# Decay factors of gated linear attention: one scan over logarithms of gates and exponentials, in place of two scans

## The chip, the cores and the metric

The kernel runs on one core of one Trainium2 chip, as one program. The metric is the device time of one execution in microseconds (us); the median over several executions is used. A core has five engines that each work through their own instructions in order: TensorE (PE in the profile, with its weight loads shown apart as PEld), VectorE (DVE), ScalarE (ACT), GpSimd (POOL) and SyncE (SP, which here only issues transfers). They wait for one another through semaphores.

## The reference

Four batches, eight heads, 768 time steps, 48 channels per head. First a gated linear attention, head by head; then, on its output with the heads laid side by side (768 x 384 per batch), a low-rank mixing over time and a two-layer network over channels.

```python
f = 1.0 / (1.0 + np.exp(-f_logit))
for t in range(S):
    state = f[:, :, t, :, None] * state + np.einsum('bhd,bhe->bhde', k[:, :, t], v[:, :, t])
    y[:, :, t] = np.einsum('bhd,bhde->bhe', q[:, :, t], state)
...
h = xt @ U @ V                      # xt: x with time and channels exchanged
u = x + h.transpose(0, 2, 1)
out = u + np.maximum(u @ w_ch1, 0.0) @ w_ch2
```

Everything is in 32-bit floats. The gates f lie between 0 and 1, one for each time step and channel.

## The kernel before

**Tiling.** A unit is a pair of heads of one batch: 16 units, numbered n = 0 to 15, four per batch. Each head takes 64 of the 128 partitions (48 channels and padding), time runs along the free dimension. The 768 steps are cut into 12 chunks of 64. Within a chunk the recurrence is written as matrix products: keys are multiplied by X, the product of the gates from the step behind theirs to the end of the chunk; queries by Y, the reciprocal of that product; scores of queries and keys, masked to the past, times values give the part from within the chunk. Between chunks a state of 48 x 48 per head is carried, scaled per chunk by the product of all its gates.

**Steps of a unit.** The function `prepare` makes X, Y, keys and queries. Units 0 to 3 (batch 0) get them from logarithms: ScalarE makes log(1 + exp(-logit)), TensorE sums it over the rest of each chunk (line 835), ScalarE takes exponentials (lines 852 to 856), and a copy (line 857) keeps the chunks' products. Units 4 to 15 (batches 1 to 3) do otherwise:

- `gates` (line 859): logits are turned so that time runs along the free dimension, by TensorE into PSUM for units 4 and 5 (line 777), by VectorE for the others (line 754, into the slice `late[6]`); ScalarE takes the sigmoid (lines 863 and 871) into a buffer `fz` whose first column of each chunk stays 0, and the sigmoid of those first columns into `f0` (lines 864 and 872). Then the load of the logits two units on is issued.
- `keep` (line 874): VectorE scans backwards over time, X[t] = f[t+1] * X[t+1] + ends[t] (line 876), then four short operations on 128 x 12 (lines 881 to 886): a copy of each chunk's product into `least`, a bound, a reciprocal into `starts`, and the chunk's whole product in `whole`.
- `keys` (line 888): the keys are turned and multiplied by X.
- `read` in `prepare`, called `read_back` where the order is written: VectorE scans forwards, Y[t] = f[t] * Y[t-1] + starts[t] (line 894).
- `queries`: the queries are turned and multiplied by Y.

The function `attend` then makes, for each unit, `kept` (keys turned back, lines 1002 to 1006, and `spread`, line 1012, which copies the chunk products to 48 columns each), `states` (line 1026, evicted by ScalarE in line 1034), `scan` (the states from chunk to chunk, on VectorE, line 1051, copied by GpSimd in line 1057 or by ScalarE in line 1055), `scores` (line 975, masked by VectorE in line 988), `read` (queries times states, line 1069, and a two-column copy `seen` on ScalarE, line 1076, which the next step waits for) and `inner` (scores times values into the same PSUM tile, line 1087, evicted by ScalarE in line 1093).

**The mixer** of a batch runs beside the attention of the next one: `ch1` (line 300) multiplies by the first weights, 12 matmuls of 256 columns into one of two PSUM banks (`ps_mm`), and ScalarE evicts with Relu (line 335); `ch2` (line 355) or a scheme with seven products (line 389) multiplies by the second weights. In the last batches a scheme with fewer products (line 495) needs many sums on VectorE (line 204, and line 929 for sums of weights).

**Weights** arrive as 64-bit words and are made into 32-bit floats while batch 0's mixer begins: two operations on ScalarE (lines 91 and 92), three on VectorE (lines 98 to 100), one addition on GpSimd (line 101) per piece.

**The order.** TensorE's instructions run in the order in which the program writes them. On VectorE and ScalarE that holds too for what is written from line 1183 to line 1306, which is batch 0, batch 1 and the first steps of unit 9's round. Instructions outside it, and all of GpSimd's, are put in order by a scheduler, which takes an instruction when, in its own model of the run, its inputs are there and its engine is free; so they may run ahead of others that stand earlier in the program. The main loop of batch 0's mixer (lines 1286 to 1292) puts behind each piece of 12 matmuls one piece of weights and then one step of the attention: gates(4), keep(4), keys(4) and so on. Later (function `steps`, line 1128), the round of unit n is: inner(n-2), scores(n-1), kept(n); from n = 7 on read_back(n) and queries(n); gates, keep and keys of n+1; then read(n-1), states(n), scan(n), with pieces of the mixer spread between by the function `Fill`.

Of the kernel before, what the change touches and what calls it, by code (L numbers as in the profile page):

```python
# [10 lines left out]
F32 = mybir.dt.float32  # L11
# [3 lines left out]
AF = mybir.ActivationFunctionType  # L15
# [549 lines left out]
def factored_path(ctx, tc, q, k, v, f_logit, moe_U, moe_V, moe_w_ch1, moe_w_ch2, out, ok):  # L565
# [135 lines left out]
    for s in range(2):  # L701
        half = causal[s * C : (s + 1) * C, :]
        nc.gpsimd.affine_select(out=half, in_=half, compare_op=ALU.is_ge, fill=0.0, base=0,
                                pattern=[[1, C]], channel_multiplier=-1)
    ends = late[:, 3, :]
    nc.vector.memset(ends, 0.0)
    nc.vector.memset(ends.rearrange("p (c t) -> p c t", t=C)[:, :, C - 1], 1.0)
    starts = other[:, 3, :]
    nc.vector.memset(starts, 0.0)
    fz = [const.tile([P, S + 1], F32, name=f"fz{i}") for i in range(2)]  # L710

    kz = [const.tile([P, C + S], F32, name=f"kz{i}") for i in range(2)]
    for i in range(2):
        nc.gpsimd.memset(kz[i][:, 0:C], 0.0)
    least = const.tile([P, NU, NCH], F32, name="least")

    wholes = [const.tile([P, NCH], F32, name=f"whole{i}") for i in range(2)]
    added = const.tile([P, D * NCH + 1], F32, name="added")
    nc.gpsimd.memset(added[:, 0:1], 0.0)
    for i in range(2):  # L720
        nc.gpsimd.memset(wholes[i][:, 0:1], 0.0)

    U = const.tile([P, NBL, R], F32, name="U")
    V = const.tile([P, (NBL * R + P - 1) // P, P], F32, name="V")
# [22 lines left out]
    def backwards(t, first, n):  # L747

        a = t[:, first : first + 1]
        return bass.AP(a.tensor, a.offset, [list(a.ap[0]), [-1, n]])  # L750

    def turned(t, src_tile):

        nc.vector.transpose(
            t.rearrange("p (c i) -> p c i", i=NB), src_tile.rearrange("p (c d) -> p c d", d=NB),
        )
# [3 lines left out]
    def prepare(n):  # L760
# [2 lines left out]
        T = units[n] = {}  # L763
        b = n // HP
        r, f = raw[n % 2], fz[n % 2]
        by_chunk = f[:, 0:S].rearrange("p (c t) -> p c t", t=C)

        def follow(nm):

            if n >= HP and n + 2 < NU:  # L770
                load(n + 2, nm)

        def on_tensor(nm):

            pt = ps_big.tile([P, 2, 512], F32, name="pt", tag="big")
            for c in range(NBL):
                nc.tensor.transpose(  # L777
                    pt[:, 2 * c // NBL, c % (NBL // 2) * P : (c % (NBL // 2) + 1) * P],
                    nat[n % 2][nm][:, c].rearrange("p h d -> p (h d)"), ident,
                )  # L780
            return pt[:, :, 0 : G * C].rearrange("p a (c t) -> p a c t", t=C)

        def halves(t):
            return t[:, 0:S].rearrange("p (a c t) -> p a c t", a=2, t=C)
# [55 lines left out]
        def keep_logs():  # L840
            def blocks_of(t):
                return t.rearrange("p (a c t) -> p a c t", a=2, t=P)

            T["X"], T["Y"] = late[:, 4 + n % 2, :], fz[n % 2][:, 0:S]
            of_least = least[:, n, :].rearrange("p (a c s) -> p a c s", a=2, s=2)
            if n == 0:
                parts = [(slice(a, a + 1), t) for a, t in enumerate(T["sums"])]
            else:
                parts = [(slice(0, 2), T["both"])]
            parts = [(a, t[:, :, 0 : NBL // 2 * (P + 2)].rearrange("p a (c t) -> p a c t", t=P + 2)) for a, t in parts]  # L850
            for a, sums in parts:
                nc.scalar.activation(blocks_of(T["X"])[:, a], sums[:, :, :, 0:P], AF.Exp, scale=-1.0)
            for a, sums in parts:
                nc.scalar.activation(blocks_of(T["Y"])[:, a], sums[:, :, :, 0:P], AF.Exp)
            for a, sums in parts:
                nc.scalar.activation(of_least[:, a], sums[:, :, :, P : P + 2], AF.Exp, scale=-1.0)
            nc.scalar.copy(wholes[n % 2][:, 1:NCH], least[:, n, 1:NCH])

        def gates():
            f0 = T["f0"] = two.tile([P, NCH], F32, name="f0")  # L860
            if n < TURNED:
                pt = on_tensor("f")
                nc.scalar.activation(halves(f)[:, :, :, 1:C], pt[:, :, :, 1:C], AF.Sigmoid)
                nc.scalar.activation(f0.rearrange("p (a c) -> p a c", a=2), pt[:, :, :, 0], AF.Sigmoid)
                follow("f")
                return
            fT = late[:, 6, :]
            turned(fT, r["f"])
            follow("f")
            fv = fT.rearrange("p (c t) -> p c t", t=C)  # L870
            nc.scalar.activation(by_chunk[:, :, 1:C], fv[:, :, 1:C], AF.Sigmoid)  # L871
            nc.scalar.activation(f0, fv[:, :, 0], AF.Sigmoid)

        def keep():
            X = T["X"] = late[:, 4, :]
            nc.vector.tensor_tensor_scan(  # L876
                backwards(X, S - 1, S), backwards(f, S, S), backwards(ends, S - 1, S), 0.0,
                ALU.mult, ALU.add,
            )
            X0 = X.rearrange("p (c t) -> p c t", t=C)[:, :, 0]  # L880
            nc.vector.tensor_copy(least[:, n, :], X0)
            X1 = two.tile([P, NCH], F32, name="X1")
            nc.vector.tensor_single_scalar(X1, X0, LEAST, ALU.max)
            nc.vector.reciprocal(starts.rearrange("p (c t) -> p c t", t=C)[:, :, 0], X1)
            whole = wholes[n % 2]
            nc.vector.tensor_tensor(whole[:, 1:NCH], T["f0"][:, 1:NCH], X0[:, 1:NCH], ALU.mult)

        def keys():
            operand("k", "X")
# [1 line left out]

        def read():
            Y = T["Y"] = late[:, 5, :]
            nc.vector.tensor_tensor_scan(Y, f[:, 0:S], starts, 0.0, ALU.mult, ALU.add)  # L894

        def queries():
            operand("q", "Y")
# [59 lines left out]
    def attend(n):  # L957
# [50 lines left out]
                spread()  # L1008

        def spread():  # L1010
            whole = T["whole"] = one.tile([P, D, NCH], F32, name="whole")
            nc.scalar.copy(whole, wholes[n % 2].unsqueeze(1).broadcast_to((P, D, NCH)))

        def halves_of(n):
            return [slice(0, D // 2), slice(D // 2, D)] if n == HP - 1 else [slice(0, D)]
# [23 lines left out]
        def scan():  # L1039

            st = T["st"] = two.tile([P, NCH, D], F32, name="st")
            by_e = "p (e c) -> p c e"
            if b == 0:
                states = st.rearrange("p c e -> p (c e)")
                T["st"] = states.rearrange(by_e, c=NCH)
            else:
                states = added[:, 0 : D * NCH]
            with tc.high_priority(offset=2 * AHEAD):
                for e in halves_of(n):
                    of = slice(e.start * NCH, e.stop * NCH)  # L1050
                    nc.vector.tensor_tensor_scan(  # L1051
                        states[:, of], added[:, of], T["whole"].rearrange("p e c -> p (e c)")[:, of], 0.0, ALU.add, ALU.mult
                    )
                if b == B - 1:
                    nc.scalar.copy(st, states.rearrange(by_e, c=NCH))
                elif b:
                    nc.gpsimd.tensor_copy(st, states.rearrange(by_e, c=NCH))  # L1057
# [125 lines left out]
    with tc.manual_schedule(engines={nc.vector.engine, nc.scalar.engine}):  # L1183
# [91 lines left out]
        m.before[4][1]()  # L1275
        ch1_of(0, 0, (0, 2), (1, 2))
        loads = loads[early + 3 :]
        for t in fz:
            nc.vector.memset(t[:, 0:S].rearrange("p (c t) -> p c t", t=C)[:, :, 0], 0.0)
            nc.vector.memset(t[:, S : S + 1], 0.0)  # L1280

        start = m.before[5:]

# [411 lines left out]
```

## Time and profile before

| | |
|---|---|
| time, median of 3 executions | 466.25 us (465.5 to 466.81) |
| span of the profiled execution, first to last instruction | 463.2 us |
| matmuls | 5639, busy 455.2 us |
| VectorE | 585 instructions, busy 351.4 us |
| ScalarE | 323 instructions, busy 170.4 us |
| GpSimd | 56 instructions, busy 48.5 us |
| granted TensorE clock, mean | 0.999 |

The profile is of one execution. A row of the timeline has start, duration (both in us), engine, line, operation, what is written and read, the number of instructions merged, and in brackets how long the engine was idle before and what released it. A row of the groups has line, engine, operation, tiles, shapes and count, then busy time in us, the mean time of one in ns, and the idle time before. A row of the windows has, for each engine, busy time and number of instructions in a stretch. Busy time of matmuls comes from modelled ends. The time of the runs lies 3.05 us above the span of the profile; that part is outside of what the profile shows.

### The profile page before, as it was taken

To read this page: it belongs to the slowest core of one execution; us is meant where nothing else is said; L and a number is where in the kernel's file an instruction comes from. 1 tells how busy PE (TensorE), PEld (TensorE's weight loads), DVE (VectorE), ACT (ScalarE), POOL (GpSimd) and SP (SyncE) were. 2 spreads that over 40 slices of the span, in tenths; PEclk is the share of its full clock that TensorE was granted. 3 is DMA by queue.
4 is the path that set the end of the run, shared out by engine and by line. 5 is a ranking of instruction groups with operands and counts; after the bars stand their busy time and mean duration, and the time that the engine had idled before them with its cause. 6 is when DMAs were issued, how large, how long until landed. Compare 5 with 4: busy or idle time off the path is not lost.

```text
span 463.2 us, 13016 instructions
## 1 busy us (share of the span) xinstructions
PE 455.2 (98%) x5639; PEld 394.5 (85%) x5639; DVE 351.4 (76%) x585; ACT 170.4 (37%) x323; POOL 48.5 (10%) x56
## 2 busy tenths in 40 slices
PE   8999999999999999999999999999999999999997
PEld 5886888875666578999898888899989999999996
DVE  6778788979999677676765559977797887858652
ACT  6785776562333143323322323451412311212200
POOL 2002445634112001010000000000000000000000
PEclk9999999999999999999999999999999999999999
DMA  9959997577777604504633030100000000000001
GB/s 194 186 139 212 227 217 180 150 119 103 124 113 118 107 18 53 78 1 89 77 52 74 14 61 4 28 3 21 18 1 1 35 1 23 13 1 35 1 36 39
DMA packets 148583, 34.35 MB, mean 74 GB/s; under 512 B 136934, under 2 KB 146982, under 8 KB 148518
## 3 DMA queue, kind: packets, MB, share of 16 engines
q1 hardware_dynamic: 147718, 33.29, 37.1%
q8 instruction: 46, 0.75, 0.7%
q10 hardware_dynamic: 800, 0.15, 0.2%
q14 instruction: 19, 0.16, 0.1%
HBM read 28.70 MB, written 4.72 MB: 72 GB/s over the span
## 4 chain that ended last, share of the span: by engine, by line
PE 80%; DVE 11%; ACT 3%; DMA 2%; issue 2%; SPq 2%; DVEq 0%; ACTq 0%
PE pw L389 27%; PE pz L300 21%; PE pp L495 12%; PE po L355 5%; PE y L1069 2%; PE sc L975 2%; PE ds L1026 2%; PE y L1087 2%; PE pt L1002 1%; SPq L661 1%; DVE late L894 1%; PE pt L777 1%; DVE late L876 1%; PE pt L835 1%; DMA other<-in_f_logit_dram 1%
## 5 line engine op out<-in xcount | busy, mean ns | idle before, releaser
L300 PE MATMUL pz<-uT,w 128*128 128x256 f32 x492 | 111.5, 382 | 0.3
L300 PEld LDWEIGHTS pz<-uT,w 128*128 128x128 f32 x492 | 91.7, 190 | 12.9 <-ACT uT L289 0.6
L389 PE MATMUL pw<-zw,w_raw 128*128 128x192 f32 x216 | 38.0, 329 | 0.0
L389 PE MATMUL pw<-w,z_all 128*128 128x192 f32 x216 | 37.3, 327 | 0.0
L335 ACT ACTIVATE z_all<-pz 128x512 f32<-128x512 f32 x33 | 19.6, 598 | 45.1 <-PE pz L300 44.7
L389 PEld LDWEIGHTS pw<-w,z_all 128*128 128x128 f32 x216 | 35.3, 190 | 0.5
L389 PEld LDWEIGHTS pw<-zw,w_raw 128*128 128x128 f32 x216 | 35.1, 190 | 0.6 <-issue 0.3
L101 POOL TENSOR_TENSOR w<-w_y,w_r 128x384 int32<-128x384 int32 x24 | 31.5, 1311 | 37.0 <-DVE w_y L100 22.5
L876 DVE TENSOR_TENSOR_SCAN late<-fz,late 128x768 f32<-128x768 f32 x12 | 21.1, 1755 | 9.4 <-ACT fz L871 9.3
L488 ACT ACTIVATE other<-other 128x512 f32<-128x512 f32 x18 | 11.3, 630 | 40.3 <-DVE other L204 40.3
L355 PE MATMUL po<-w,zw 128*128 128x384 f32 x72 | 25.2, 495 | 0.0
L355 PE MATMUL po<-w,z_all 128*128 128x384 f32 x72 | 24.7, 493 | 0.0
L1057 POOL COPY st<-added 128x576 f32<-128x576 f32 x8 | 12.4, 1556 | 113.8 <-DVE added L1051 113.8
L988 DVE TENSOR_TENSOR A<-sc,causal 128x768 f32<-128x768 f32 x16 | 15.2, 953 | 8.5 <-PE sc L975 8.5
L355 PEld LDWEIGHTS po<-w,zw 128*128 128x128 f32 x72 | 13.2, 190 | 9.6 <-issue 0.8
L894 DVE TENSOR_TENSOR_SCAN late<-fz,other 128x768 f32<-128x768 f32 x12 | 21.0, 1750 | 0.2
L355 PEld LDWEIGHTS po<-w,z_all 128*128 128x128 f32 x72 | 13.3, 190 | 8.9 <-DVE o L204 0.6
L488 ACT ACTIVATE z_all<-z_all 128x512 f32<-128x512 f32 x12 | 7.6, 631 | 34.1 <-DVE z_all L204 34.1
L1034 ACT COPY added<-ds 48x576 f32<-48x576 f32 (+2 forms) x29 | 17.8, 619 | 4.5 <-PE ds L1026 4.1
L495 PE MATMUL pp<-v_nat,late 128*128 128x128 f32 x152 | 19.1, 275 | 0.0
L1069 PEld LDWEIGHTS y<-st,qT 48*64 48x64 f32 x704 | 13.6, 137 | 6.2 <-issue 4.5
L98 DVE TENSOR_SCALAR w_y<-w_y 128x384 f32<-128x384 f32 (+3 forms) x27 | 12.1, 449 | 8.8 <-ACT w_y L91 8.8
(233 smaller groups left out, 872.1 us busy)
## 6 DMA issues: line engine op xcount, KB each, us to landing
w_raw<-in_moe_w_ch_dram SPq DMA_DIRECT2D x18, 384.0 KB, 3.6
out_dram<-o SPq DMA_DIRECT2D x17, 192.0 KB, 1.9
v_nat<-in_v_dram SPq DMA_DIRECT2D x16, 144.0 KB, 3.8
v_nat<-in_v_dram SPq DMA_DIRECT2D x32, 72.0 KB, 3.5
zw<-in_moe_w_ch_dram SPq DMA_DIRECT2D x6, 384.0 KB, 5.1
out_dram<-o SPq DMA_DIRECT2D x14, 96.0 KB, 2.2
w<-in_k_dram SPq DMA_DIRECT2D x4, 288.0 KB, 4.1
w<-in_q_dram SPq DMA_DIRECT2D x4, 288.0 KB, 4.2
```

The costliest lines, as they stand in the source:

```text
L101: nc.gpsimd.tensor_tensor(dst.bitcast(I32), shaped(y.bitcast(I32)), shaped(r), ALU.add)
L300: nc.tensor.matmul(pm[:, i * 2 * P : (i + 1) * 2 * P], lhsT=w1[:, m, o : o + P], rhs=uT[a][:, m, :], start=(m == 0), stop=(m == NDC - 1))
L335: nc.scalar.activation(z[a, c][:, k : k + 2, :].rearrange("p i t -> p (i t)"), pm, AF.Relu)
L355: nc.tensor.matmul(pm, lhsT=z[a, i // NI][:, i % NI, s * P : (s + 1) * P], rhs=w2[:, i, :], start=(i == 0), stop=(i == NFC - 1))
L389: nc.tensor.matmul(W["pm"][:, n * HM : (n + 1) * HM], lhsT=lhs[:, i, :], rhs=rhs[:, i, :], start=(i == 0), stop=(i == NI - 1))
L488: nc.scalar.activation(dst, dst, AF.Relu, scale=float(SIGNS[n]))
L495: nc.tensor.matmul(pm[:, i, r * P : (r + 1) * P], lhsT=room["w"](wn)[:, r * P : (r + 1) * P], rhs=x_node(a, xn), start=((xn, wn) == of[0]) ...
L876: nc.vector.tensor_tensor_scan(backwards(X, S - 1, S), backwards(f, S, S), backwards(ends, S - 1, S), 0.0, ALU.mult, ALU.add,)
L894: nc.vector.tensor_tensor_scan(Y, f[:, 0:S], starts, 0.0, ALU.mult, ALU.add)
L988: nc.vector.tensor_tensor(T["A"], sc[:, :, 0 : NBL * C].rearrange("p h (c i) -> p h c i", i=C), causal.unsqueeze(1).unsqueeze(1).broadcast ...
L1034: nc.scalar.copy(added[r, 1:].rearrange("p (e c s) -> p e c s", c=NBL, s=2)[:, e], ds[r, :, 0 : NBL * D].rearrange("p s (c e) -> p e c s", ...
L1069: nc.tensor.matmul(o(c % 2, par, c // 2), lhsT=T["q"][rows[par], chunk[c]], rhs=T["st"][rows[par], c, :], start=(c <= 2), stop=False, skip ...
```

## The change

For units 4 to 15 the gates stay logarithms until after the scan. GpSimd first bounds the logits from below by -40, in place. They are turned as before; ScalarE takes exp(-logit) and then log(1 + ...), in place, over all 768 columns. One backward scan on VectorE, in place, sums these over the rest of each chunk (`within` is 1, and 0 in each chunk's last column). ScalarE then takes X as the exponential of minus the sum, the chunks' products straight into `least`, and, in place of the second scan, Y as the exponential of the sum. The bound, the reciprocal and the product on 128 x 12 are gone; last columns of X and Y are set to 1 once. In batch 0 the copy of line 857 is gone, since `spread` reads `least`.

```diff
--- before.py
+++ after.py
@@ -702,23 +702,20 @@
         half = causal[s * C : (s + 1) * C, :]
         nc.gpsimd.affine_select(out=half, in_=half, compare_op=ALU.is_ge, fill=0.0, base=0,
                                 pattern=[[1, C]], channel_multiplier=-1)
-    ends = late[:, 3, :]
-    nc.vector.memset(ends, 0.0)
-    nc.vector.memset(ends.rearrange("p (c t) -> p c t", t=C)[:, :, C - 1], 1.0)
-    starts = other[:, 3, :]
-    nc.vector.memset(starts, 0.0)
-    fz = [const.tile([P, S + 1], F32, name=f"fz{i}") for i in range(2)]
+    within = late[:, 3, :]
+    nc.vector.memset(within, 1.0)
+    nc.vector.memset(within.rearrange("p (c t) -> p c t", t=C)[:, :, C - 1], 0.0)
+    fz = [const.tile([P, S], F32, name=f"fz{i}") for i in range(2)]
 
     kz = [const.tile([P, C + S], F32, name=f"kz{i}") for i in range(2)]
     for i in range(2):
         nc.gpsimd.memset(kz[i][:, 0:C], 0.0)
     least = const.tile([P, NU, NCH], F32, name="least")
 
-    wholes = [const.tile([P, NCH], F32, name=f"whole{i}") for i in range(2)]
+    whole = const.tile([P, D, NCH], F32, name="whole")
+    nc.gpsimd.memset(whole[:, :, 0], 0.0)
     added = const.tile([P, D * NCH + 1], F32, name="added")
     nc.gpsimd.memset(added[:, 0:1], 0.0)
-    for i in range(2):
-        nc.gpsimd.memset(wholes[i][:, 0:1], 0.0)
 
     U = const.tile([P, NBL, R], F32, name="U")
     V = const.tile([P, (NBL * R + P - 1) // P, P], F32, name="V")
@@ -763,7 +760,9 @@
         T = units[n] = {}
         b = n // HP
         r, f = raw[n % 2], fz[n % 2]
-        by_chunk = f[:, 0:S].rearrange("p (c t) -> p c t", t=C)
+
+        def by_chunk(t):
+            return t.rearrange("p (c t) -> p c t", t=C)
 
         def follow(nm):
 
@@ -841,7 +840,7 @@
             def blocks_of(t):
                 return t.rearrange("p (a c t) -> p a c t", a=2, t=P)
 
-            T["X"], T["Y"] = late[:, 4 + n % 2, :], fz[n % 2][:, 0:S]
+            T["X"], T["Y"] = late[:, 4 + n % 2, :], f
             of_least = least[:, n, :].rearrange("p (a c s) -> p a c s", a=2, s=2)
             if n == 0:
                 parts = [(slice(a, a + 1), t) for a, t in enumerate(T["sums"])]
@@ -854,36 +853,25 @@
                 nc.scalar.activation(blocks_of(T["Y"])[:, a], sums[:, :, :, 0:P], AF.Exp)
             for a, sums in parts:
                 nc.scalar.activation(of_least[:, a], sums[:, :, :, P : P + 2], AF.Exp, scale=-1.0)
-            nc.scalar.copy(wholes[n % 2][:, 1:NCH], least[:, n, 1:NCH])
 
         def gates():
-            f0 = T["f0"] = two.tile([P, NCH], F32, name="f0")
+            raw_f = nat[n % 2]["f"][:, :, :, 0:D] if n < TURNED else r["f"]
+            nc.gpsimd.tensor_single_scalar(raw_f, raw_f, FLOOR, ALU.max)
             if n < TURNED:
-                pt = on_tensor("f")
-                nc.scalar.activation(halves(f)[:, :, :, 1:C], pt[:, :, :, 1:C], AF.Sigmoid)
-                nc.scalar.activation(f0.rearrange("p (a c) -> p a c", a=2), pt[:, :, :, 0], AF.Sigmoid)
-                follow("f")
-                return
-            fT = late[:, 6, :]
-            turned(fT, r["f"])
+                nc.scalar.activation(halves(f), on_tensor("f"), AF.Exp, scale=-1.0)
+            else:
+                turned(f, r["f"])
+                nc.scalar.activation(f, f, AF.Exp, scale=-1.0)
             follow("f")
-            fv = fT.rearrange("p (c t) -> p c t", t=C)
-            nc.scalar.activation(by_chunk[:, :, 1:C], fv[:, :, 1:C], AF.Sigmoid)
-            nc.scalar.activation(f0, fv[:, :, 0], AF.Sigmoid)
+            nc.scalar.activation(f, f, AF.Ln, bias=1.0)
 
         def keep():
+            nc.vector.tensor_tensor_scan(
+                backwards(f, S - 1, S), backwards(within, S - 1, S), backwards(f, S - 1, S), 0.0, ALU.mult, ALU.add,
+            )
             X = T["X"] = late[:, 4, :]
-            nc.vector.tensor_tensor_scan(
-                backwards(X, S - 1, S), backwards(f, S, S), backwards(ends, S - 1, S), 0.0,
-                ALU.mult, ALU.add,
-            )
-            X0 = X.rearrange("p (c t) -> p c t", t=C)[:, :, 0]
-            nc.vector.tensor_copy(least[:, n, :], X0)
-            X1 = two.tile([P, NCH], F32, name="X1")
-            nc.vector.tensor_single_scalar(X1, X0, LEAST, ALU.max)
-            nc.vector.reciprocal(starts.rearrange("p (c t) -> p c t", t=C)[:, :, 0], X1)
-            whole = wholes[n % 2]
-            nc.vector.tensor_tensor(whole[:, 1:NCH], T["f0"][:, 1:NCH], X0[:, 1:NCH], ALU.mult)
+            nc.scalar.activation(by_chunk(X)[:, :, 0 : C - 1], by_chunk(f)[:, :, 1:C], AF.Exp, scale=-1.0)
+            nc.scalar.activation(least[:, n, :], by_chunk(f)[:, :, 0], AF.Exp, scale=-1.0)
 
         def keys():
             operand("k", "X")
@@ -891,7 +879,7 @@
 
         def read():
             Y = T["Y"] = late[:, 5, :]
-            nc.vector.tensor_tensor_scan(Y, f[:, 0:S], starts, 0.0, ALU.mult, ALU.add)
+            nc.scalar.activation(by_chunk(Y)[:, :, 0 : C - 1], by_chunk(f)[:, :, 1:C], AF.Exp)
 
         def queries():
             operand("q", "Y")
@@ -1008,8 +996,7 @@
                 spread()
 
         def spread():
-            whole = T["whole"] = one.tile([P, D, NCH], F32, name="whole")
-            nc.scalar.copy(whole, wholes[n % 2].unsqueeze(1).broadcast_to((P, D, NCH)))
+            nc.scalar.copy(whole[:, :, 1:], least[:, n, 1:].unsqueeze(1).broadcast_to((P, D, NCH - 1)))
 
         def halves_of(n):
             return [slice(0, D // 2), slice(D // 2, D)] if n == HP - 1 else [slice(0, D)]
@@ -1049,7 +1036,7 @@
                 for e in halves_of(n):
                     of = slice(e.start * NCH, e.stop * NCH)
                     nc.vector.tensor_tensor_scan(
-                        states[:, of], added[:, of], T["whole"].rearrange("p e c -> p (e c)")[:, of], 0.0, ALU.add, ALU.mult
+                        states[:, of], added[:, of], whole.rearrange("p e c -> p (e c)")[:, of], 0.0, ALU.add, ALU.mult
                     )
                 if b == B - 1:
                     nc.scalar.copy(st, states.rearrange(by_e, c=NCH))
@@ -1275,9 +1262,8 @@
         m.before[4][1]()
         ch1_of(0, 0, (0, 2), (1, 2))
         loads = loads[early + 3 :]
-        for t in fz:
-            nc.vector.memset(t[:, 0:S].rearrange("p (c t) -> p c t", t=C)[:, :, 0], 0.0)
-            nc.vector.memset(t[:, S : S + 1], 0.0)
+        for i in range(4, 6):
+            nc.vector.memset(late[:, i, :].rearrange("p (c t) -> p c t", t=C)[:, :, C - 1], 1.0)
 
         start = m.before[5:]
 
```

## The prediction

> **What bounds the kernel now.** I read the page first: the busy times and the chain that ended last.
>
> ```profile
> span 463.2 us, 13016 instructions
> PE 455.2 (98%) x5639; PEld 394.5 (85%) x5639; DVE 351.4 (76%) x585; ACT 170.4 (37%) x323; POOL 48.5 (10%) x56
> PE 80%; DVE 11%; ACT 3%; DMA 2%; issue 2%; SPq 2%; DVEq 0%; ACTq 0%
> ```
>
> TensorE is busy for 455.2 of 463.2 us and holds 80% of the chain; VectorE holds 11%. The change takes work from VectorE, so the question is where TensorE waits for VectorE. The windows view answers it by stage (for each engine busy time and count, then clock, DMA share and GB/s):
>
> ```profile
> 48.00:440.00 392.00, 390.76 (x4506) 339.73 (x4505) 308.39 (x494) 136.78 (x248) 40.88 (x29) 1.00 0.34 63
> 100.00:145.00 45.00, 44.21 (x834) 28.87 (x833) 40.21 (x55) 15.90 (x32) 8.26 (x5) 1.00 0.79 115
> ```
>
> From 48 to 440 us, where all of the changed units run, TensorE is idle for 392.00 - 390.76 = 1.24 us. Waits of TensorE that end earlier can give no more than that. Of it, 45.00 - 44.21 = 0.79 us lie between 100 and 145 us, where VectorE too is nearly full (40.21 of 45). A gain must come from there; a loss can come from anywhere that a new wait reaches TensorE.
>
> Busy time of matmuls is modelled, so I checked the pace in the densest part of that stretch, with the chain and the group of weight loads:
>
> ```profile
> 134.68 7.94 PE po L355 x24
> ```
>
> ```profile
> L355 PEld LDWEIGHTS po<-w,zw 128*128 128x128 f32 x72 | 13.2, 190 | 9.6 <-issue 0.8
> ```
>
> 7.94 / 24 = 0.33 us per matmul against 0.19 us for the load of its weights: the matmul hides the load, and a dense run of these shows the loads busy only 57% of the time. The Trainium skill (Trainium Kernel Development and Optimization, Performance Expectations) says that matmul busy time is a bad measure of nearness to the limit, since matmuls are pipelined, and that weight-load busy time is a good one; in this stretch that is 28.87 of 45, and by that rule TensorE would have room and VectorE would be the bound. The 57% of a dense run speaks against it here; the case is a rival below.
>
> **The change, part by part.** What leaves and what comes, from the groups by line:
>
> ```profile
> L876 DVE TENSOR_TENSOR_SCAN late<-fz,late 128x768 f32<-128x768 f32 x12 | 21.1, 1755 | 9.4 <-ACT fz L871 9.3
> L894 DVE TENSOR_TENSOR_SCAN late<-fz,other 128x768 f32<-128x768 f32 x12 | 21.0, 1750 | 0.2
> L881 DVE COPY least<-late 128x12 f32<-128x12 f32 x12 | 3.9, 326 | 0.4
> L884 DVE RECIPROCAL other<-X 128x12 f32<-128x12 f32 x12 | 2.8, 230 | 0.2
> ```
>
> ```profile
> L871 ACT ACTIVATE fz<-late 128x756 f32<-128x756 f32 x10 | 8.3, 832 | 20.2 <-DVE late L754 20.2
> L825 ACT ACTIVATE other<-other 128x576 f32<-128x576 f32 x2 | 1.4, 686 | 0.0
> L857 ACT COPY whole<-least 128x11 f32<-128x11 f32 x4 | 0.8, 199 | 0.1
> ```
>
> ```profile
> L101 POOL TENSOR_TENSOR w<-w_y,w_r 128x384 int32<-128x384 int32 x24 | 31.5, 1311 | 37.0 <-DVE w_y L100 22.5
> L1057 POOL COPY st<-added 128x576 f32<-128x576 f32 x8 | 12.4, 1556 | 113.8 <-DVE added L1051 113.8
> ```
>
> VectorE loses, per unit, the scan of 1.75 us and four short operations, two of which are 0.33 and 0.23: together over 2.3 us, 28 us over 12 units. Beside full matmuls that is worth nothing by itself. ScalarE gets four passes of about 0.83 us (exponential, logarithm, X, Y) for one sigmoid of 0.83, so 2.5 us per unit and 30 us in all; it is busy 37%, so its time costs nothing, its order may. That a logarithm costs what an exponential does I take from line 825: 0.69 us at 576 columns beside 0.83 at 756.
>
> The bound on GpSimd is not in the trace. Below it stands the two-input addition of 384 columns (1.3 us), above it the strided copy of 576 scaled to 768 (2.1 us); I take 1.7, nearer to the copy, which has one input too. Its cover is the time between a load's landing and the turn of the logits, and the loads are issued two units ahead. GpSimd's order is the scheduler's, and that it pulls instructions forward is seen on VectorE, where unit 10's second scan ran ahead of the mixer's additions, which stand earlier in the program:
>
> ```profile
> 158.66 1.76 DVE L894 TENSOR_TENSOR_SCAN late<-fz,other 128x768 f32<-128x768 f32 x1
> 160.34 2.66 DVE L204 TENSOR_TENSOR x<-x,pu 128x768 f32<-128x768 f32 x3
> ```
>
> So I put it at 0. The load two units on is issued behind the turn, as before.
>
> *First unit.* Unit 4's steps stand between pieces of the mixer:
>
> ```profile
> 55.24 0.82 PE L777 MATMUL pt<-ident,late 128*128 128x128 f32 x6
> 58.18 1.28 ACT L863 ACT_TABLE_LOAD   x1
> 60.01 1.00 POOL L101 TENSOR_TENSOR w<-w_y,w_r 128x384 int32<-128x384 int32 x1 [0.95 <-DVE w_y L100]
> 60.23 0.61 ACT L335 ACTIVATE z_all<-pz 128x512 f32<-128x512 f32 x1
> 61.60 0.61 ACT L335 ACTIVATE z_all<-pz 128x512 f32<-128x512 f32 x1
> 61.73 5.34 PE L300 MATMUL pz<-uT,w 128*128 128x256 f32 x24
> 62.09 0.56 DVE L100 SCALAR_TENSOR_TENSOR w_y<-w_raw,w_y 128x384 uint32<-128x384 uint32 x1
> 62.56 1.75 DVE L876 TENSOR_TENSOR_SCAN late<-fz,late 128x768 f32<-128x768 f32 x1
> 62.80 2.31 POOL L101 TENSOR_TENSOR w<-w_y,w_r 128x384 int32<-128x384 int32 x1 [1.79 <-ACT w_y L91]
> ...
> 102.16 0.83 ACT L871 ACTIVATE fz<-late 128x756 f32<-128x756 f32 x1 [1.85 <-DVE late L754]
> 103.01 0.55 ACT L91 ACTIVATE w_y<-w_raw 128x384 f32<-128x384 f32 x1
> ```
>
> The table load goes, and with it the sigmoid; from 58.18 to the eviction at 60.23 are 2.05 us, now two passes of 0.83, which overlap a little: 1.5. All that follows is 0.5 earlier, the scan at 62.05 instead of 62.56, its end at 63.8. But X now stands on ScalarE ahead of the eviction that was at 61.60, and waits for the scan. X and the short pass behind it take 0.85 (as the sigmoids do from 102.16 to 103.01), the eviction 0.6: done at 65.25. Of the 24 matmuls from 61.73 the second dozen starts after half of 5.34, at 64.4, and needs that PSUM bank. **New wait: 0.9 us.** Queued behind X are that eviction and the weights' two passes; at unit 5 the eviction comes late too, and I count no second wait. Y comes later on ScalarE, and the queries' product waits for it in the place of the scan; it has that scan's 1.75 us to come in.
>
> GpSimd's additions take 1.00 us at 60.01 and 2.31 at 62.80, beside the scan; a bound that meets a scan just ahead of the last addition for the weights (below) could cost up to 2.3 there, and that goes into the range. The Trainium skill (GPSIMD Engine Reference, Engine selection and Key points) would leave an elementwise max on VectorE, and says that GpSimd shares its SBUF interfaces with VectorE, with contention when that has two SBUF inputs; by that rule, with which these two rows agree, the bound is put on the wrong engine, and the sum would be the range's 2.3 higher.
>
> *Last weights.* At unit 6, behind the two rows of 102.16 and 103.01:
>
> ```profile
> 105.09 2.31 POOL L101 TENSOR_TENSOR w<-w_y,w_r 128x384 int32<-128x384 int32 x1 [2.72 <-DVE w_y L100]
> 107.45 0.30 PEld L355 LDWEIGHTS po<-w,zw 128*128 128x128 f32 x2 [0.62 <-POOL w L101]
> ```
>
> TensorE already waits there for the last piece of weights. The logarithm stands ahead of that piece's pass of 103.01: 0.83, less the short sigmoid that goes, so 0.6, and the chain to 107.45 moves with it. **0.6 us more.**
>
> *Rounds of units 6 to 9.* Where VectorE is full:
>
> ```profile
> 115.91 0.76 PE L1026 MATMUL ds<-v_nat,kb 64*48 64x48 f32 x48 [0.57 <-issue]
> 117.59 1.76 DVE L876 TENSOR_TENSOR_SCAN late<-fz,late 128x768 f32<-128x768 f32 x1 [0.90 <-ACT fz L871]
> 129.71 0.14 ACT L1076 COPY seen<-y 128x2 f32<-128x2 f32 x1
> 129.72 1.76 DVE L876 TENSOR_TENSOR_SCAN late<-fz,late 128x768 f32<-128x768 f32 x1 [0.90 <-ACT fz L871]
> 132.25 0.92 PE L1087 MATMUL y<-v_nat,A 64*64 64x48 f32 x48
> 134.10 0.58 PE L1002 MATMUL pt<-ident,kz 64*128 64x64 f32 x12 [0.21 <-DVE kz L805]
> ```
>
> A round of VectorE takes 129.72 - 117.59 = 12.13 us. It loses 1.75 and about 0.45 of the short operations, which partly overlap, and gets 0.85 of waiting for the logarithm: 1.35 us less. The two waits of TensorE, 0.57 and 0.21, have VectorE's backlog behind them; I let both go. **0.8 us less.** Next in line is the copy `seen`, for which the matmuls at 132.25 wait: it stood behind the sigmoid and now stands behind X. With VectorE no further ahead it would end 0.85 + 1.76 + 1.05 after 129.72, at 133.4, or 1.15 too late; with two rounds' lead of 1.35 each it is in time. I count nothing, and the rest is a rival.
>
> *Batch 0 and the rest.* The copy of line 857, four of 0.2 us, goes from ScalarE's order; the step behind it mostly waits for TensorE: 0.1 less, between 0 and 0.8. Cleared buffers at the start lie before the first loads land. Behind 145 us TensorE hardly waits: 0.
>
> **Sum** against the profiled execution: 463.2 + 0.9 + 0.6 - 0.8 - 0.1 = 463.8. The median of the runs, 466.25, lies 3.05 above the span, so 466.25 + 0.6, 466.8 us.
>
> **The rivals.**
>
> *VectorE is the bound between 100 and 145 us.* For it: weight loads busy 28.87 of 45 us there (64%), VectorE 40.21 (89%). Against: 0.79 us of idle TensorE, and its pace. Three rounds between the scans of units 6 to 9 would each be 1.35 shorter, 4.0 in place of 0.8: 463.6 us.
>
> *ScalarE held behind the scan.* In the hand-written order X, waiting for VectorE, holds back `seen` and the evictions behind it, in each round. For it: TensorE has no slack, and unit 4 shows the same trap. Against: VectorE's 1.35 per round. It decides when VectorE gains less than 1.15 us before unit 8. Three rounds of 1.15 give 3.5: 470.3, and half of that 468.5.
>
> *GpSimd in program order.* If bounds are not pulled forward, unit 4's turn at 55.24 waits behind the addition at 60.01, which stands earlier in the program: 60.01 + 1.00 + 1.7 - 55.24 = 7.5 us, 474. Against it is the scan at 158.66.
>
> **How the numbers follow.** A measurement of this kernel can tell about 0.3%, 1.4 us, from no change, so "same" is 464.85 to 467.65. My forecast has 0.50, VectorE as the bound 0.13, ScalarE held 0.24, GpSimd's order 0.05; the 0.08 left, for accidents of the scheduler in batches 2 and 3, I split evenly. Faster 0.17, same 0.50, slower 0.33. The range leaves out the faster rival's lower half and the slowest cases: 464.4 to 470.0, which holds the unknown costs of the forecast too (waits of 1.24 all gone and no new one: 464.9; a bound ahead of the last weights: 469.1). The likeliest case alone: 465.2 to 467.6.
>
> **What would show it.** Right: VectorE some 28 us less busy, ScalarE some 30 more, no table load at 58 us, TensorE idle for about 0.9 us between unit 4's dozens of line 300 and again at the last weights, and no wait at 115.91 and 134.10. Wrong: TensorE idle before line 1087 round after round (ScalarE held), before line 777 (GpSimd), or rounds of 10.8 us with TensorE's pace unchanged but fewer gaps (VectorE as the bound). More than 1.4 us to either side would make the forecast wrong.

## The result, and the profile after

The changed kernel takes 470.18 us (median of 4 executions, 469.06 to 471.61), 3.9 us more than the 466.25 of before; the ratio is 1.0086, with a 95% interval of 1.0061 to 1.0112. The forecast was 466.8, with 470.0 as the range's upper end: the change is slower by more than its measurement is uncertain, and by far more than the 0.6 us foreseen. The profiled execution took 469.32 us.

First the head of the page of the changed kernel, and the engines' shares of the chain that ended last.

```profile
span 467.6 us, 13029 instructions
...
PE 455.8 (97%) x5639; PEld 394.9 (84%) x5639; DVE 322.7 (69%) x522; ACT 196.5 (42%) x354; POOL 68.0 (15%) x67
...
PE 85%; DVE 5%; ACT 3%; DMA 2%; issue 2%; POOL 1%; SPq 1%; DVEq 0%; POOLq 0%; ACTq 0%
```

VectorE is 28.7 us less busy (351.4 to 322.7), ScalarE 26.1 more, GpSimd 19.5 more; the busy time of TensorE is the same within 0.6. So the work went where the change sent it. Of the 4.4 us by which the span is longer, 3.8 are idle time of TensorE: 467.6 - 455.8 = 11.8 us, against 463.2 - 455.2 = 8.0 before. Most of it lies in the longer of the two stretches that the prediction used (busy time and count of each engine, then clock, DMA share and GB/s):

```profile
48.00:440.00 392.00, 387.14 (x4480) 335.56 (x4479) 276.43 (x429) 162.45 (x281) 59.32 (x41) 1.00 0.35 63
100.00:145.00 45.00, 44.23 (x731) 29.27 (x720) 33.28 (x38) 25.84 (x44) 15.23 (x10) 1.00 0.81 116
```

TensorE is now idle for 4.86 of the 392 us, where it was 1.24. Between 100 and 145 us, where VectorE fell from 40.21 to 33.28, TensorE gained nothing on the whole; its 0.77 us of idle time there are now the wait for the last weights. What it waited for in the stretch from 48 to 440 us (total, times, longest) says where. The names are the PSUM tiles that TensorE writes: `pz` the product with the first weights, `po` the one with the second, `ds` the states, `pt` and `pu` turned blocks and the low-rank part. Before:

```profile
PE ds L1026 <- issue: 0.6, 1, 0.6
PE pt L1002 <- DVE kz L805: 0.2, 1, 0.2
PE pu L214 <- DVE x L204: 0.2, 1, 0.2
```

After:

```profile
PE pz L300 <- ACT z_all L335: 3.6, 2, 2.1
PE po L355 <- POOL w L101: 0.8, 1, 0.8
```

The waits at units 6 to 9 are gone, as forecast. Two waits on evictions in the first unit and one at the last weights have come. The start of the same TensorE instruction in the two traces shows when the loss arises:

| TensorE instruction | before, us | after, us | later by |
|---|---|---|---|
| turn of unit 4's logits | 55.24 | 55.82 | 0.58 |
| first dozen of line 300 behind unit 4's second turn | 61.73 | 64.03 | 2.30 |
| second dozen | 64.33 | 68.94 | 4.61 |
| first `po` of the last weights | 103.95 | 108.67 | 4.72 |
| `inner` behind the last weights | 108.29 | 113.78 | 5.49 |
| first `ds` of the next round | 115.91 | 120.56 | 4.65 |
| span | 463.2 | 467.6 | 4.4 |

4.0 us arise in the 13 us from the first turn to the second dozen, 0.8 at the last weights, and 0.8 is won back at `ds`. Of batch 1's changed steps only unit 4's bound lies ahead of the 0.58 at the top (at 45.15 us on GpSimd), and runs 5 and 6, which have no bound, come to this turn at 56.31 and 56.38. I leave it as scatter: in the three series of runs below, 67 executions of the kernel before had spans from 462.9 to 467.8.

The first unit in the timeline of the changed kernel (start, duration, and in brackets the idle time before and what ended it):

```profile
58.18 1.64 POOL L859 TENSOR_SCALAR other<-other 128x576 f32<-128x576 f32 x1 [2.45 <-DMA other<-in_f_logit_dram]
...
59.79 1.96 POOL L101 TENSOR_TENSOR w<-w_y,w_r 128x384 int32<-128x384 int32 x2
...
60.82 0.57 ACT L91 ACTIVATE w_y<-w_raw 128x384 f32<-128x384 f32 x1 [3.55 <-POOL w L101]
...
61.74 0.79 ACT L861 ACTIVATE fz<-pt 128x768 f32<-128x768 f32 x1
...
62.56 0.84 ACT L866 ACTIVATE fz<-fz 128x768 f32<-128x768 f32 x1
...
63.31 0.58 ACT L335 ACTIVATE z_all<-pz 128x512 f32<-128x512 f32 x1
...
64.03 2.83 PE L300 MATMUL pz<-uT,w 128*128 128x256 f32 x12 [1.55 <-ACT z_all L335]
...
65.62 1.75 DVE L869 TENSOR_TENSOR_SCAN fz<-late,fz 128x768 f32<-128x768 f32 x1
...
67.46 0.83 ACT L873 ACTIVATE late<-fz 128x756 f32<-128x756 f32 x1 [2.70 <-DVE fz L869]
68.20 0.20 ACT L874 ACTIVATE least<-fz 128x12 f32<-128x12 f32 x1
68.31 0.58 ACT L335 ACTIVATE z_all<-pz 128x512 f32<-128x512 f32 x1
...
68.94 2.86 PE L300 MATMUL pz<-uT,w 128*128 128x256 f32 x12 [2.09 <-ACT z_all L335]
...
78.19 0.82 PE L776 MATMUL pt<-ident,other 128*128 128x128 f32 x6
```

Read it from the top. The first row is the bound of unit 5, the next unit, whose logits TensorE turns only at 78.19, 20 us later. GpSimd waits 2.45 us for their load and works 1.64 us on them; behind it, in the same queue, stands an addition that makes weights, at 59.79. In the trace of before that addition is here:

```profile
56.11 1.00 POOL L101 TENSOR_TENSOR w<-w_y,w_r 128x384 int32<-128x384 int32 x1 [0.96 <-DVE w_y L100]
```

59.79 - 0.58 - 56.11 = 3.1 us late. ScalarE's next pass over weights waits for it (60.82, idle for 3.55), and behind that pass, in order, stand unit 4's exponential, its logarithm and the eviction at 63.31, for which TensorE waits 1.55 us. The scan starts late with them, X (67.46) waits for the scan, the next eviction stands behind X: 2.09 us more.

### The profile page after: what moved, and what is told of

It reads as the page before. It is cut to its first block, busy times and chain, and to the rows that moved or that the text cites. A ratio compares the mean times of both kernels' runs of the same rounds, so it can differ in the third digit from the quotient of the medians.

```text
span 467.6 us, 13029 instructions
## 1 busy us (share of the span) xinstructions
PE 455.8 (97%) x5639; PEld 394.9 (84%) x5639; DVE 322.7 (69%) x522; ACT 196.5 (42%) x354; POOL 68.0 (15%) x67
## 3 DMA queue, kind: packets, MB, share of 16 engines
HBM read 28.70 MB, written 4.72 MB: 71 GB/s over the span
## 4 chain that ended last, share of the span: by engine, by line
PE 85%; DVE 5%; ACT 3%; DMA 2%; issue 2%; POOL 1%; SPq 1%; DVEq 0%; POOLq 0%; ACTq 0%
PE pw L389 27%; PE pz L300 19%; PE pp L495 12%; PE po L355 9%; PE y L1056 3%; PE y L1074 2%; DMA other<-in_f_logit_dram 2%; PE sc L963 2%; PE ds L1013 2%; PE pt L990 2%; PE pt L834 1%; PE pt L776 1%; POOL w L101 1%; PE idle L1177 1%; ACT w_y L91 1%
## 5 line engine op out<-in xcount | busy, mean ns | idle before, releaser
L869 DVE TENSOR_TENSOR_SCAN fz<-late,fz 128x768 f32<-128x768 f32 x12 | 21.1, 1755 | 19.5 <-ACT fz L866 19.5
L101 POOL TENSOR_TENSOR w<-w_y,w_r 128x384 int32<-128x384 int32 x24 | 28.8, 1203 | 31.5 <-DVE w_y L100 16.9
L1044 POOL COPY st<-added 128x576 f32<-128x576 f32 x8 | 9.8, 1224 | 100.9 <-DVE added L1038 100.9
L204 DVE TENSOR_TENSOR w_raw<-z_all 128x768 f32<-128x768 f32 x12 | 11.4, 952 | 11.7 <-ACT z_all L335 10.3
L873 ACT ACTIVATE late<-fz 128x756 f32<-128x756 f32 x12 | 10.0, 833 | 22.2 <-DVE fz L869 20.6
L1038 DVE TENSOR_TENSOR_SCAN added<-added,whole 128x576 f32<-128x576 f32 x12 | 16.3, 1356 | 4.3 <-ACT added L1021 4.3
```

What stands on the lines that cost most here:

```text
L101: nc.gpsimd.tensor_tensor(dst.bitcast(I32), shaped(y.bitcast(I32)), shaped(r), ALU.add)
L869: nc.vector.tensor_tensor_scan(backwards(f, S - 1, S), backwards(within, S - 1, S), backwards(f, S - 1, S), 0.0, ALU.mult, ALU.add,)
L1038: nc.vector.tensor_tensor_scan(states[:, of], added[:, of], whole.rearrange("p e c -> p (e c)")[:, of], 0.0, ALU.add, ALU.mult)
```

## The experiments

**Theory 1, GpSimd's order:** the scheduler put unit 5's bound ahead of additions of weights, where it waits for a load. **Theory 2, ScalarE's order:** X, which waits for the scan, stands ahead of an eviction; the bound is cheap. The forecast had 0.9 us for the second and nothing for the first. Each kernel was timed beside the kernel before on the same chip, in three series, in which the kernel before took 466.11, 466.25 and 466.51 us.

**1. The bound on VectorE.**

```diff
-            nc.gpsimd.tensor_single_scalar(raw_f, raw_f, FLOOR, ALU.max)
+            nc.vector.tensor_single_scalar(raw_f, raw_f, FLOOR, ALU.max)
```

> The kernel after, with the bound of the logits on VectorE in place of GpSimd. Theory 1 (GpSimd's order: unit 5's bound stands ahead of an addition of weights, waits there for its load, and everything behind it on ScalarE comes late): TensorE's wait of 1.55 us ahead of unit 4's first dozen goes, and of the second wait of 2.09 only the 0.9 of the forecast stays, so 470.2 - 1.55 - 1.2 = 467.4 us. Theory 2 (ScalarE's order: X, which waits for the scan, stands ahead of an eviction): the second wait stays whole and only some of the first goes, 469.0 us or more.

Measured: 480.09 us, ratio 1.0286 (1.0267 to 1.0306). Neither theory had this. TensorE's waits from 48 to 440 us, and the first bound in the timeline:

```profile
PE pt L776 <- DVE late L859: 4.9, 1, 4.9
PE pt L776 <- DVE other L859: 2.9, 1, 2.9
PE po L355 <- POOL w L101: 1.4, 1, 1.4
...
```

```profile
61.89 0.45 DVE L859 TENSOR_SCALAR late<-late 128x576 f32<-128x576 f32 x1
```

The same bound takes 0.45 us here and 1.64 on GpSimd, so the engine is the better one; the place is far worse. VectorE's order is the written one in this stretch, the bound stands in `gates` just ahead of its turn, behind several pieces of weights, and TensorE waits for it twice. The experiment changed the place along with the engine, so it doesn't decide between the theories. It does show, on another engine, the case of the third rival, a bound in program order. Not all of its 14 us are waits: its five executions have a mean clock of 0.986 to 0.993, so by estimate (1 - 0.993) x 477.6 = 3.3 to (1 - 0.986) x 479.1 = 6.7 us of them went with the clock. The rule of the Trainium skill that the prediction weighed (GPSIMD Engine Reference, Engine selection: an elementwise maximum belongs on VectorE) is by itself no guide here: followed without regard to the place it costs 10 us more than the changed kernel.

**2. X of units 4 and 5 one step later** (the edit, shortened):

```diff
 def keep():
     ...
-            nc.scalar.activation(X[...], f[...], AF.Exp, scale=-1.0)
-            nc.scalar.activation(least[...], f[...], AF.Exp, scale=-1.0)
 def keys():
+            # units 4 and 5 only; the others keep them in keep()
+            nc.scalar.activation(X[...], f[...], AF.Exp, scale=-1.0)
+            nc.scalar.activation(least[...], f[...], AF.Exp, scale=-1.0)
     operand("k", "X")
```

> The kernel after, with the bound still on GpSimd, but at units 4 and 5 the exponentials of X and of least go from the scan's step to the head of the keys' step, behind one more piece of the mixer. Theory 1: the wait of 1.55 us for the bound stays and so does part of the second, so 468.2 to 469 us. Theory 2: both waits go for the most part, since both are evictions behind X: about 466.8 us.

Measured: 467.72 us, 1.0042 (1.0023 to 1.0060), between the two. The waits:

```profile
PE pz L300 <- ACT z_all L335: 1.0, 1, 1.0
PE po L355 <- POOL w L101: 0.8, 1, 0.8
```

The wait of 2.09 is gone whole, the first is 1.05 in the place of 1.55. Of that half a microsecond 0.44 is not the edit's: TensorE came to unit 4's first turn that much later in this execution (56.26 against 55.82) and had less to wait for the same load. So X ahead of the eviction carries the second wait, as theory 2 has it, and the bound the first, as theory 1 has it.

**3. Both edits.**

> The two edits together: bound on VectorE, X and least of units 4 and 5 in the keys' step. Both theories: no wait of TensorE at unit 4, 470.2 - 1.55 - 2.09 = 466.5 us. If a part of the two waits has another cause, 467.5 us or more.

Measured: 479.6 us, 1.0295 (1.0273 to 1.0317). The waits of 4.9 and 2.9 for VectorE's bound are there as in the first run, and hide whatever the second edit gives: a miss, for the same reason.

**4. The bound alone, in the kernel before.** One line at the head of `gates`, all else as before: two scans, the sigmoid.

> The kernel before, with the bound alone added: a maximum of each unit's logits on GpSimd ahead of its turn, for units 4 to 15, and all the rest as it was (two scans, the sigmoid on ScalarE). GpSimd's order is then the one of the kernel after. Theory 1: unit 5's bound waits for its load here too and holds the addition behind it: some 1.5 to 2.5 us more than before, 468 to 468.7 us. Theory 2: GpSimd has room, no change, 466.3 us.

Measured: 469.78 us, 1.0081 (1.0068 to 1.0095). This one line, with nothing else of the change, costs 3.7 us. GpSimd's order comes out as in the changed kernel at unit 5's bound, and TensorE's two largest waits are:

```profile
PE pz L300 <- ACT z_all L335: 1.6, 1, 1.6
PE po L355 <- POOL w L101: 0.9, 1, 0.9
...
```

**5. No bound from unit 4 on.**

> The kernel after, with the bound of the logits left out at units 4 to 15 (a part of the computation is missing; GpSimd has only the weights' additions and the copies of st). Theory 1: what the bound costs is gone, on GpSimd and for those who wait for it: TensorE's 1.55 us ahead of unit 4's first dozen, and of the 2.09 behind it all but the forecast's 0.9, so 470.2 - 2.7 = 467.5 us. Theory 2, if ScalarE's order makes both waits: 469 us or more.

Measured: 467.12 us, 1.0015 (0.9999 to 1.0031), as theory 1 had it. What is left of TensorE's waits:

```profile
PE pz L300 <- ACT z_all L335: 1.0, 1, 1.0
PE po L355 <- POOL w L101: 0.8, 1, 0.8
```

```profile
66.53 2.86 PE L300 MATMUL pz<-uT,w 128*128 128x256 f32 x12 [0.97 <-ACT z_all L335]
```

That one wait on the eviction, 0.97 us, is the forecast's 0.9 for X.

**6. No bound, and X later.**

> The bound left out at units 4 to 15 and X and least of units 4 and 5 in the keys' step. Both theories, as a sum of two parts: no wait of TensorE at unit 4 is left, 467.5 - 0.9 = 466.6 us or a little less. If the waits overlap, the gain of the second edit is 0 and it stays at 467.5 us.

Measured: 465.77 us, 0.9988 (0.9972 to 1.0003). The wait of 0.97 us is gone, and so are 1.35 us of time; the intervals of runs 5 and 6 cover the difference.

**7. The bounds of units 4 and 5 on VectorE, ahead of their need** (the edit, partly in words):

```diff
 def queries():                       # unit 4
     operand("q", "Y")
     follow("q")
+            bound of unit 5          # nc.vector
     ...
+        bound of unit 4              # nc.vector, ahead of the loop over the mixer's pieces
```

> The kernel after, with the bounds of units 4 and 5 alone on VectorE, at places written by hand ahead of their need (unit 4's ahead of the loop over the mixer's pieces, unit 5's behind unit 4's product of the queries), all others on GpSimd as they were. Theory 1 (unit 5's bound in GpSimd's order is what costs, the others are hidden): like the kernel without bounds, 467.5 us. If GpSimd's other bounds cost too (beside scans, ahead of the last weights): 468.5 us or more. If VectorE's bounds hold up TensorE's turns wherever they stand: 472 us or more.

Measured: 466.91 us, 1.0016 (1.0001 to 1.0031), the same as with no bound at all, with ten bounds still on GpSimd. Those ten, one of them ahead of the last weights, cost nothing that can be seen; the place on VectorE is what made 480 of the first run.

**8. That, and X later, and unit 6's logarithm behind the last weights' passes** (line 866 at the head of `keep` for unit 6).

> As the run before, and X and least of units 4 and 5 in the keys' step, and unit 6's logarithm behind the last weights' passes on ScalarE. If the three causes (GpSimd's order, X ahead of the eviction, the logarithm ahead of the last weights) make the whole loss: 470.2 - 1.55 - 2.09 - 0.6 = 465.9 us, at or just under the time before. If the forecast's 0.8 of TensorE's waits at units 6 to 9 is gained as well as measured: the same 465.9, with no wait of TensorE over 0.3 us between 48 and 145 us. If something else costs: 467 us or more.

Measured: 465.65 us, 0.9989 (0.9973 to 1.0006). The wait for the last weights halves:

```profile
PE po L355 <- POOL w L101: 0.4, 1, 0.4
```

In time that cannot be seen beside run 6. With the change's waits mended but for these 0.4 us, TensorE is idle for 392.00 - 391.15 = 0.85 us of the long stretch and VectorE still 26 us less busy than before, yet the time is that of the kernel before:

```profile
48.00:440.00 392.00, 391.15 (x4509) 340.22 (x4508) 283.02 (x435) 164.80 (x284) 57.52 (x40) 1.00 0.34 63
```

**9. The bound at unit 5 alone, on GpSimd.**

> The kernel after with the bound at unit 5 alone, on GpSimd, where it stands between the sixth and the seventh addition of the first weights as in the kernel after; at units 4 and 6 to 15 it is left out (a part of the computation is missing). If this one bound is the whole loss of the bound: TensorE's waits of 1.5 and 2.1 us at unit 4 are back, 470 us. If the twelve bounds share the loss: about 467.5 us, near the kernel without bounds (467.1).

Measured: 471.0 us, 1.0101 (1.0086 to 1.0117). One bound of twelve brings the whole loss back:

```profile
PE pz L300 <- ACT z_all L335: 3.1, 2, 2.1
...
```

**10. Unit 5's load earlier**: its issue moved ahead of four loads of weights.

> The kernel after with the load of unit 5's logits issued ahead of four loads of weights instead of behind them, some 2 us earlier; the scheduler of GpSimd then puts the bound three additions earlier too. If the wait for the load is what costs, and the order goes by a forecast of the landing that is too early: the bound waits again, now ahead of the fourth addition, and the loss stays, 469 to 471 us. If only the 1.6 us of the bound's own time cost, or the later landing: the three additions more make up for it, 468 us or less.

Measured: 469.44 us, 1.0070 (1.0057 to 1.0084). The scheduler moved the bound up with the load, to the place behind the third addition:

```profile
52.78 1.65 POOL L859 TENSOR_SCALAR other<-other 128x576 f32<-128x576 f32 x1 [3.55 <-DVE w_y L100]
...
54.39 1.96 POOL L101 TENSOR_TENSOR w<-w_y,w_r 128x384 int32<-128x384 int32 x2
```

GpSimd is idle for 3.55 us in front of it again. (The row names VectorE as the releaser; the bound reads nothing but its load, which I take to be what it waited for.) The first wait is gone in this kernel, the second is 2.3 us. An earlier load alone doesn't mend it, since the order follows the load.

**11. All bounds on GpSimd, its order written by hand**: unit 4's bound behind the third addition, each later one behind the queries of the unit ahead of it.

> The kernel after with all bounds on GpSimd, but GpSimd's order written by hand like ScalarE's and VectorE's: unit 4's bound behind the third addition, that of each later unit behind the product of the queries of the unit ahead of it. If the place is what costs and not the engine: like the run with units 4 and 5 on VectorE, 467 us. If the bound's 1.6 us costs on GpSimd wherever it stands: 468.5 us or more.

Measured: 467.97 us, 1.0034 (1.0023 to 1.0046): between the two. The place gives back 2.2 of the 3.1 us that the bound costs; 0.85 stay. I put them down to the engine, where unit 4's bound still puts 1.65 us into the chain of weights; the wait on the second eviction is 1.4 here against 1.0 without a bound, but the intervals of runs 5 and 11 overlap, and no run separates it further.

**12. That, and X later.**

> As the run before, and X and least of units 4 and 5 in the keys' step: the whole of the change with the two orders mended. Place theory: 465.8 us, no difference from the kernel before that can be measured. Engine theory: 467.2 us or more.

Measured: 466.56 us, 1.0003 (0.9994 to 1.0012). The whole change, bound on GpSimd included, costs nothing once the two places are mended, and it gains nothing. No run beats the kernel before by what can be told.

## Why the prediction was wrong, point by point

**What bounds the kernel: right.** The prediction said that taking 28 us from VectorE is worth nothing by itself beside full matmuls. Runs 6, 8 and 12 show that: VectorE is at 325.4 us in run 8 against 351.4 before, and the three ratios are 0.9988, 0.9989 and 1.0003.

**The bound on GpSimd "at 0": this step failed.** Its duration was put a little low (1.7 us estimated for 768 columns; the trace has 2.1 for 768, and 1.64 for the 576 of unit 5), which is not what cost. What failed is the reasoning on its cover. The prediction asked when the bound is needed and found time enough, and took it as a good sign that the scheduler pulls instructions forward. The question to ask was what stands behind it on GpSimd's queue where it lands. It was pulled forward to 20 us before its need, to a place where its load had not landed, ahead of additions on which ScalarE's evictions depend. The upper end of 2.3 us was placed at the last weights. There the wait is 0.8 us with the bound and without it (runs 7 and 5); the cost arose with the first weights. From the changed kernel to run 5 the ratio falls by 0.0071, 3.3 us, which is nearly the whole miss: 466.8 + 3.3 = 470.1. About 1 us of it is not wait but clock (last section).

The third rival named the same two queues, with the sign reversed: a bound that comes too late for TensorE. It came too early for GpSimd. Run 1 made the late case, on another engine: 4.9 us of wait at unit 4, where 7.5 had been worked out.

**First unit, 0.9 us: right**, in mechanism and size, once the bound is away: 0.97 us in run 5, and 1.35 us of time from run 5 to run 6. With the bound in place the same trap took 2.09, since the scan came later still: the two costs aren't independent. Run 2 alone gave back 2.5 us and run 5 alone 3.1; both together (run 6) gave 4.4, not 5.6.

**Last weights, 0.6 us: right in the trace** (later by 5.49 - 4.72 = 0.77 there), for the reason given: run 8 moved the logarithm, and the wait fell from 0.8 to 0.4. What is left in run 8 can be put down to the bound of unit 7, from its rows:

```profile
102.95 2.20 POOL L859 TENSOR_SCALAR other<-other 128x768 f32<-128x768 f32 x1
...
104.50 0.85 DVE L99 TENSOR_SCALAR w_y<-w_y 128x384 uint32<-128x384 uint32 x1
```

Line 99 is a VectorE pass on the last weights. It takes 0.85 us beside the bound, and 0.36 at the same place before (103.99) and in run 6, which has no bound; the 0.49 more are enough for the wait of 0.40. In run 4, with no logarithm there, the same pass takes 0.85 beside the bound too, and the matmuls wait 0.93 us for the last weights, where before only the weight load ahead of them did (0.62 at 107.45). So the bound does have a cost at the last weights, of about half a microsecond, which the logarithm hides in the changed kernel. No run takes it apart by itself.

**Rounds of units 6 to 9, 0.8 less: right** (5.49 - 4.65 = 0.84).

**Batch 0, 0.1 less: can't be told.** The turn of unit 4's logits comes at 55.24 us in the one profile before and at 55.82 to 56.84 in the profiles of changed kernels in which it waits for nothing; scatter of this size hides 0.1.

**ScalarE held behind the scan, round after round: did not happen.** This is `seen` in the round for which the prediction worked out 1.15 us (the matmuls that stood at 132.25 before):

```profile
135.29 0.83 ACT L873 ACTIVATE late<-fz 128x756 f32<-128x756 f32 x1 [1.82 <-DVE fz L869]
...
136.15 0.14 ACT L1063 COPY seen<-y 128x2 f32<-128x2 f32 x1
...
136.94 0.92 PE L1074 MATMUL y<-v_nat,A 64*64 64x48 f32 x48
```

ScalarE does wait for the scan, but `seen` ends 0.65 us before the matmuls that wait for it. That rival's 470.3 is close to the result by chance; its mechanism is not in the trace of the changed kernel. It is near, though: in runs 11 and 12 TensorE waits for `seen` once, 0.2 us, and in run 1 twice, 0.8 us together.

**VectorE as the bound from 100 to 145 us: refuted** by run 8. That rival gave 463.6, 2.6 us less than before, with the new waits in it; run 8 has VectorE relieved and the new waits mended but for 0.4 us, and lies within 1.3 us of before by its interval. The dense run's 57%, against which the prediction weighed the Trainium skill's rule on weight-load busy time (Trainium Kernel Development and Optimization, Performance Expectations), was the better guide here.

**From span to time.** The prediction took all 3.05 us between the span and the median as lying outside the span. In every execution of the later runs 1.7 to 1.8 us lie outside (469.32 - 467.6 = 1.72 in the changed kernel's profile); by that the profiled execution before took about 464.9 us, 1.3 under its median. The sum was added to the median, so the forecast isn't touched.

## What to carry to other kernels

An operation put on an idle engine can cost what stands behind it in that engine's queue, at the place where the scheduler puts it: ask where it lands, whether its input is there by then, and which engines wait for the next instruction in the queue. The same holds for a cheap pass moved to an engine with a written order, where it can hold back an eviction that TensorE waits for. Before giving an engine relief, ask whether any wait of the bounding engine ends on it; here 1.24 us was all that could be had, and 28 us of relief bought none that can be measured.

## What the runs showed of the hardware

A lower TensorE clock came behind short waits. In run 9 TensorE waits twice in the first unit:

```profile
63.83 2.83 PE L300 MATMUL pz<-uT,w 128*128 128x256 f32 x12 [1.04 <-ACT z_all L335]
68.76 4.28 PE L300 MATMUL pz<-uT,w 128*128 128x256 f32 x12 [2.10 <-ACT z_all L335]
```

The windows from there on show the granted clock (third number from the end) at 0.51 and 0.64 for 4 us:

```profile
66.00:70.00 4.00, 1.90 (x10) 1.34 (x9) 1.94 (x4) 2.72 (x7) 1.97 (x1) 1.00 0.47 130
70.00:72.00 2.00, 2.00 (x7) 1.55 (x6) 1.97 (x4) 1.71 (x4) 1.00 (x1) 0.51 0.18 35
72.00:74.00 2.00, 2.00 (x10) 1.70 (x9) 0.84 (x2) 0.92 (x2) 0.98 (x1) 0.64 0.49 169
74.00:76.00 2.00, 2.00 (x11) 1.75 (x10) 1.77 (x4) 0.57 (x2) 0.37 (x2) 1.00 0.81 214
```

2 x 0.49 + 2 x 0.36 = 1.7 us are lost by it. All four executions of run 9 have a mean clock of 0.995 to 0.996. So have two of the four of the changed kernel, at 471.04 and 471.61 us, against 469.06 and 469.32 at 1.00: its median holds about 1 us of this. The waits are not the only road to a lower clock: 5 of the 67 executions of the kernel before had 0.989 to 0.996 too, and no profile shows where they lost it. The Trainium skill (TensorE: Matmul & The Clock Gate, HAM oscillation — how this bites in real kernels) warns of idle gaps above some 3.4 us; in run 9 no wait between 56 and 72 us was longer than 2.10, with 2.8 us of matmuls between the two, and the measurement decides; in the changed kernel the like waits, 1.55 and 2.09, stand in an execution that kept a clock of 1.00.

An in-place maximum of 128 x 576 took 1.64 us on GpSimd (the row of 58.18) and 0.45 on VectorE (run 1): 3.6 times as long for an operation with one input.

A VectorE pass that meets a GpSimd operation can be held until that one is done. Line 99's pass over 128 x 384, 0.36 us elsewhere, took 1.06 at 56.27 in the kernel before and 0.85 in runs 4 and 8, and ended 0.2 us behind the GpSimd operation each time (57.33 against 57.11, 107.57 against 107.36, 105.35 against 105.15). The prediction looked for such a meeting in one direction alone, GpSimd's additions slowed beside a scan.
